# One written-out order of 1,100 steps, replaced by another, in a two-way attention followed by a two-layer network

## The chip, the core and the metric

The kernel runs on one core of one Trainium2 chip. The metric is the device time of one execution in microseconds (us). Five engines take part: TensorE (PE, matrix products, with its weight loads shown as PEld), VectorE (DVE), ScalarE (ACT), GpSimd (POOL), and SyncE (SP), which only issues transfers. Each engine runs its own queue strictly in the order of the program; where an instruction waits, all behind it in that queue wait too. Three runs of the kernel before took 209.22, 209.41 and 210.38 us, with a median of 209.41 us.

## The reference

```python
def _attn_ref(x, state):                     # x: 8 x 8 x 512 x 64, state: 8 x 8 x 32 x 64
    scale = 1.0 / np.sqrt(D)
    scores = scale * np.matmul(x, state.transpose(0, 1, 3, 2))
    a = softmax(scores)                      # over the 32 states
    xread = np.matmul(a, state)
    scores2 = scale * np.matmul(state, x.transpose(0, 1, 3, 2))
    a2 = softmax(scores2)                    # over the 512 tokens
    sread = np.matmul(a2, x)
    return np.concatenate([xread, sread], axis=2)

def reference(...):                          # rows: 8 x (512 + 32) = 4352, width 512
    x = attn_out.transpose(0, 2, 1, 3).reshape(B * S, H * D)
    h = x @ w_in                             # 512 x 2048
    g = np.maximum(h, 0.0) + alpha * np.minimum(h, 0.0)
    return g @ w_out                         # 2048 x 512
```

(`softmax` stands here for the lines that subtract the maximum, take the exponential and divide by the sum.)

## The kernel before

All work is cut into small steps, and one string, `ORDER`, lists them. A loop at the end of the kernel reads the string from front to back and calls the function of each step, so the list fixes the order of instructions on every engine at once. Nothing is moved by a scheduler afterwards. A step's name is followed by its numbers; a trailing letter names the engine (`a` ACT, `v` DVE, `p` POOL), and a trailing digit of a step on PE names the PSUM bank (0 to 5) that its result takes. Two more banks form one double tile called `two`.

The steps that matter here, with b a batch (0 to 7; 8 stands for the state rows of all batches together):

- `lst`, `wi`, `wo`, `lx`: transfers that POOL issues: the states, a quarter of `w_in` (512 columns), a quarter of `w_out` (512 rows), the tokens x of a batch. They convert 32-bit to 16-bit numbers on the way. x of batch 0 comes by transfers of SP and ACT instead, and `cx` casts it.
- `xt`/`xo`, `str`/`sro`: transposes on PE of x and of the states, and the copy out of PSUM. Later batches have `xd`, a transposing transfer on SP, in place of `xt`/`xo`.
- `tsc` or `sc`: scores on PE. `smax`, `ssh`, `sexp`, `ssum`, `snorm`, `wb`: the softmax over the states (largest of 32, subtract, exponential, sum and reciprocal, multiply, transpose back); for batch 0 in two halves, with `at`/`ao` (transposes on PE and copies) in place of `wb`. `tm`, `nb`, `te`, `tsum`, `tn`, `tt`: the softmax over the tokens, `rd`/`rdo` its product with x.
- `m.b.f`/`mo`: the states times a quarter f of `w_in`, on PE, and the copy to 16 bits. Since xread = a @ state, x @ w_in is got as a @ (state @ w_in).
- `F.b.jc`: 128 of the 2048 hidden columns for the 512 tokens of a batch (two matmuls 128x512; `f` the same in halves for the first two columns of batch 0). `N` on ACT takes relu(-h), `G` on DVE forms g = h + (1 - alpha) * relu(-h) (`n` and `g` for the halves).
- `S.0.q.j`/`O`: the second product of batch 0, in four PSUM banks. For batches 1 to 8 a product of 2x2 blocks with seven block products is used in place of eight: `W` (POOL, once) forms differences of blocks of `w_out`, `U.b.i.c` (POOL) sums and differences of blocks of g, `P.b.p.i.c` (PE) the seven products, `K` a copy of a partial sum from PSUM, `Q` the last addition or copy of an output block and its transfer by SP.
- `Z.k.n`: matmuls on a constant pattern whose result nobody reads; n counts 256 columns each. `fill(0, 16)` ahead of the list issues eight of 128x512.

What waits for what follows from the tiles. `F.b` needs the weights of its batch (`wb.b`, or `ao` for batch 0) and the `mo` of its quarter; `S` needs the `G` of two columns; `P` needs `G` or `U`; a step on PE that takes a bank waits until the last reader of what stood there is through.

Of the kernel before, what the change touches and what calls it, by code (L numbers as in the profile page):

```python
# [18 lines left out]
lst.0 cx.0.1.v cx.0.0.a xt.0.0.0.0 stc.a stt.1 cx.1.0.v sbd.1.a sto.a sbd.0.a xt.0.0.1.2 xt.0.1.0.3 xo.0.1.0.a  # L19
xo.0.0.0.v Z.4.3 xo.0.0.1.v tsc.0.1.4 cx.1.1.v tsc.0.0 smax.0.0 ssh.v.0.0 xt.0.1.1.5 xo.0.1.1.a sexp.0.0 tsc.1.0.0  # L20
Z.1.9 tsc.1.1 str.0.1 wi.0 m.0.0.2.3 sro.0.a Z.5.6 smax.0.1 ssh.v.0.1 Z.5.6 m.2.0.5.4 lx.1 sexp.0.1 m.1.0 mo.0.0.a.0
la mo.0.0.a.1 ssum.0.0 wi.1 mo.1.0.a ssum.0.1 wo.0 mo.2.0.v.1 snorm.p.0.0 xt.1.1.0.0 xt.1.0.0.1 xt.1.1.1.2 xo.1.1.0.a
xt.1.0.1.3 at.0.4 ao.0.a xo.1.0.0.v snorm.p.0.1 Z.1.3 xo.1.0.1.v oma.a xo.1.1.1.v at.1.1 sc.1 f.0.0.0.3 ao.1.a wi.2
F.0.3.0 F.0.2.2 m.0.1.4.1 mo.2.0.a.0 Z.5.3 n.0.0.0 f.0.0.1.5 N.0.3 mo.0.1.a.0 sb.1 tm.1 mo.0.1.a.1 F.0.7.4 F.0.5.1
N.0.2 g.0.0.0.1 g.0.0.0.0 G.0.2 n.0.0.1 G.0.3 g.0.0.1.1 nb.1.a te.1.0 g.0.0.1.0 N.0.7 N.0.5 F.0.6.3 G.0.7 smax.1
S.0.0.0.2 G.0.5 te.1.1 F.0.4.0 S.0.0.1 S.0.3.1.5 wo.1 wi.3 S.0.3.0 tsum.1 N.0.6 m.0.2 mo.0.2.a wo.2 S.0.1.1.4 wo.3
W.1.0.p G.0.6 S.0.1.0 m.1.1 F.0.10.1 N.0.4 G.0.4 mo.1.1.a N.0.10 G.0.10 F.0.8.3 S.0.1.3 S.0.1.2 ssh.p.1 sexp.1
F.0.9.0 ssum.1.s N.0.9 lx.2 xd.2 S.0.0.3 N.0.8 G.0.8 F.0.11.1 N.0.11 S.0.3.3 W.1.1.p snorm.p.1 m.0.3 mo.0.3.a S.0.3.2
# [5 lines left out]
sb.2 m.2.2.0.1 rd.1.2 mo.2.2.a.0 mo.2.2.a.1 rdo.1.a tm.2 S.0.3.7 tt.0 smax.2 S.0.3.5 O.0.3.a N.1.13 S.0.2.1.2 nb.2.a
S.0.2.5 te.2.1 S.0.2.6 S.0.2.7 te.2.0 F.1.1.0 N.1.1 G.1.13 F.1.8.1 N.1.8 G.1.0 G.1.1 F.1.4.5 S.0.2.2 m.3.2 G.1.8
N.1.4 G.1.4 F.1.10.0 lx.3 ssh.p.2 lst.1 sexp.2 mo.3.2.a ssum.2.1 tsum.2 S.0.2.4 S.0.2.0 F.1.9.5 rd.0.3 P.1.2.0.1.4
snorm.v.2 rdo.0.a N.1.9 G.1.9 S.0.2.3 N.1.10 P.1.1.0.1.3 P.1.1.1.1 P.1.2.1.1 xd.3 O.0.2.a tn.2.0.a m.2.3.1.2
mo.2.3.a.0 m.2.1 mo.2.3.a.1 wb.2 G.1.10 F.1.11.5 N.1.11 mo.2.1.a G.1.11 P.1.1.1.0 U.1.1.1.p str.1.1 sro.1.v tn.2.1.p
# [5 lines left out]
P.1.5.0.0 smax.3 P.1.7.1.1.4 F.2.10.1 N.2.10 F.2.5.0 N.2.5 G.2.5 G.2.10 F.2.4.2 N.2.4 G.2.4 te.3.1 P.1.5.1.1
U.1.3.0.p P.1.7.1.0 P.1.5.0.1 K.1.4.a U.1.4.1.p F.2.3.5 N.2.3 G.2.3 P.1.7.0.1 F.2.6.0 N.2.6 ssh.p.3 lx.5 F.2.12.1
N.2.12 G.2.6 P.1.7.0.0 P.1.3.1.0 m.6.0 Q.1.1.1 m.4.1.2.5 sexp.3 P.1.3.1.1 mo.6.0.a G.2.12 mo.4.1.a.0 ssum.3.0
U.2.1.0.p snorm.v.3 P.1.3.0.0 P.1.4.0.0 mo.4.1.a.1 P.1.3.0.1 U.2.2.0.p Q.1.0.1.a P.1.4.1.1 tsum.3 m.6.1.1.2 wb.3
mo.6.1.a.0 m.4.3 mo.4.3.a m.5.3.5.3 P.1.4.0.1 mo.5.3.a.1 P.2.1.0.1.1 P.2.1.1.0 P.1.4.1.0 mo.5.3.a.0 sc.4 U.2.1.1.p
# [772 lines left out]
```

## Time and profile before

| | |
|---|---|
| median of three runs | 209.41 us (209.22 to 210.38) |
| the profiled execution: span from its first to its last instruction | 207.1 us |
| PE busy | 200.4 us, 97% of the span |
| POOL busy | 179.5 us, 87% |
| DVE busy | 171.7 us, 83% |
| ACT busy | 155.3 us, 75% |
| first `F` with 512 columns (F.0.3) starts | 15.07 us |

The profile shows one execution, the span of which is given; its own time is not stated beside the span, so the 2.3 us between span and median are what lies around it. In a row of the timeline the columns are start, duration, engine, line, operation, output and inputs with their shapes, and the number of instructions merged into the row; a bracket tells how long the engine was idle before it, and for what. Matmul durations overlap: dense 128x512 matmuls start every 0.216 us though each is shown as 0.38 us long. "waited for" rows give total, times and longest.

### The profile page before, as it was taken

Reading aid. Unit: us, or ns where it says so; the run is one execution under the profiler, and the core shown is the slowest. Engines: PE = TensorE matmul, PEld = TensorE weight load, DVE = VectorE, ACT = ScalarE, POOL = GpSimd, SP = SyncE. Lnnn points to the kernel's source line nnn. Section 1 sums busy time; section 2 is a strip of 40 time slices with the busy share of each in tenths; the row PEclk is TensorE's granted clock in tenths of the full one; section 3 lists DMA queues with packets and bytes.
Section 4 is the critical chain, followed back from the end, with each engine's and each line's share of the span. In section 5 each row is a group of like instructions: output and inputs, shape, how many; then the busy total and the mean of one; then the engine's idle time right before and its main releaser. Section 6 shows DMA issues by size and latency. Waiting matters only on the chain.

```text
span 207.1 us, 5034 instructions
## 1 busy us (share of the span) xinstructions
PE 200.4 (97%) x1997; PEld 133.6 (65%) x1997; DVE 171.7 (83%) x251; ACT 155.3 (75%) x306; POOL 179.5 (87%) x113
## 2 busy tenths in 40 slices
PE   7899999999999999999999999999999999999992
PEld 2553344445566656687667856776877687788882
DVE  0889899999999999999999999999987967733231
ACT  4699999998999999997899787968755757502120
POOL 8177789997998999997997999797997999999960
PEclk9999999999999999999999999999999999999998
DMA  6999996698928798238976530126101200023223
GB/s 175 215 207 205 204 204 97 158 173 106 178 82 101 116 192 156 53 38 167 243 118 104 148 105 0 54 103 152 55 0 53 102 0 3 0 101 104 101 77 125
DMA packets 44038, 23.68 MB, mean 114 GB/s; under 512 B 22256, under 2 KB 43504, under 8 KB 44016
## 3 DMA queue, kind: packets, MB, share of 16 engines
q1 hardware_dynamic: 31152, 14.82, 28.4%
q0 software_dynamic: 11792, 8.09, 27.3%
q10 hardware_dynamic: 1072, 0.46, 0.9%
q8 instruction: 15, 0.25, 0.4%
q14 instruction: 7, 0.06, 0.1%
HBM read 17.31 MB, written 8.91 MB: 127 GB/s over the span
## 4 chain that ended last, share of the span: by engine, by line
PE 86%; DVE 5%; ACT 4%; DMA 2%; issue 1%; ACTq 0%
PE px L736 26%; PE h L577 24%; PE pv L736 13%; PE py L736 7%; PE m_ps L528 4%; PE h L586 3%; PE o L647 3%; DVE g L633 3%; DMA x<-in_x_dram 2%; PE sr_ps L501 2%; PE fill L253 2%; ACT neg L630 1%; PE sc L335 1%; ACT m L554 1%; PE xT_ps L320 1%
## 5 line engine op out<-in xcount | busy, mean ns | idle before, releaser
L633 DVE SCALAR_TENSOR_TENSOR g<-neg,oma_sb,h 128x512 f16<-128x512 f32 (+1 forms) x142 | 94.0, 711 | 11.6 <-ACT neg L630 11.0
L630 ACT ACTIVATE neg<-h 128x512 f32<-128x512 f32 (+1 forms) x142 | 75.6, 580 | 16.5 <-PE h L577 11.5
L577 PE MATMUL h<-aT,m 128*128 128x512 f16 x252 | 66.8, 380 | 0.1
L736 PEld LDWEIGHTS <-gsum 128*128 128x128 f16 x480 | 46.5, 98 | 13.1 <-issue 0.9
L736 PEld LDWEIGHTS <-g 128*128 128x128 f16 x360 | 34.7, 98 | 8.8 <-issue 1.4
L715 POOL TENSOR_TENSOR gsum<-g,g 128x1024 f16<-128x1024 f16 (+1 forms) x16 | 32.1, 2007 | 6.7 <-DVE g L633 4.9
L577 PEld LDWEIGHTS <-m 128*128 128x128 f16 x252 | 23.8, 98 | 18.4 <-issue 2.0
L715 POOL TENSOR_TENSOR gsum<-g,gsum 128x1024 f16<-128x1024 f16 (+1 forms) x16 | 32.0, 2005 | 1.5 <-PE px L736 1.0
L715 POOL TENSOR_TENSOR gsum<-gsum,g 128x1024 f16<-128x1024 f16 (+1 forms) x16 | 32.1, 2007 | 1.0
L736 PE MATMUL px<-ws,gsum 128*128 128x256 f16 x240 | 32.1, 273 | 0.0
L715 POOL TENSOR_TENSOR gsum<-g 128x1024 f16<-128x1024 f16 (+1 forms) x16 | 31.9, 2006 | 0.0
L752 ACT COPY kept<-px 128x512 f32<-128x512 f32 (+1 forms) x24 | 13.6, 567 | 21.0 <-PE px L736 20.9
L554 ACT CAST m<-m_ps 128x512 f16<-128x512 f32 x35 | 19.1, 602 | 1.5 <-PE m_ps L528 1.1
L769 DVE TENSOR_TENSOR oq<-pv,kept 128x512 f32<-128x512 f32 (+1 forms) x16 | 10.4, 649 | 10.6 <-PE pv L736 10.4
L736 PE MATMUL px<-w_out_sb,gsum 128*128 128x256 f16 x120 | 17.2, 273 | 0.0
L736 PE MATMUL px<-w_out_sb,g 128*128 128x256 f16 x120 | 17.2, 273 | 0.0
L405 POOL TENSOR_TENSOR ts<-ts,mx 128x1024 f32<-128x1024 f32 x7 | 13.3, 1911 | 4.4 <-DVE mx L400 4.4
L647 PE MATMUL o<-w_out_sb,g 128*128 128x512 f16 x64 | 16.6, 380 | 0.1
L736 PE MATMUL py<-w_out_sb,g 128*128 128x256 f16 x120 | 16.6, 273 | 0.0
L736 PE MATMUL pv<-ws,gsum 128*128 128x256 f16 x120 | 16.4, 273 | 0.0
L736 PE MATMUL pv<-ws,g 128*128 128x256 f16 x120 | 15.9, 273 | 0.0
L552 ACT CAST m<-m_ps 128x1024 f16<-128x1024 f32 x13 | 13.2, 1018 | 0.5 <-PE m_ps L528 0.4
(75 smaller groups left out, 238.1 us busy)
## 6 DMA issues: line engine op xcount, KB each, us to landing
out_dram<-oq SPq DMA_DIRECT2D x28, 256.0 KB, 2.6
xg<-in_x_dram POOLq DMA_DIRECT2D x7, 512.0 KB, 7.4
w_in_sb<-in_moe_w_in_dram POOLq DMA_DIRECT2D x4, 512.0 KB, 8.6
w_out_sb<-in_moe_w_out_dram POOLq DMA_DIRECT2D x4, 512.0 KB, 12.7
out_dram<-osb SPq DMA_DIRECT2D x4, 256.0 KB, 2.9
x<-in_x_dram SPq DMA_DIRECT2D x2, 256.0 KB, 3.7
out_dram<-oq SPq DMA_DIRECT2D x4, 128.0 KB, 2.1
x<-in_x_dram ACTq DMA_DIRECT2D x1, 256.0 KB, 4.6
```

The source lines that it names most:

```text
L405: engine(e).tensor_tensor(blocks(cols(live["ts", b], j, S)), blocks(scored(b, j)), over_blocks(cols(live["mx", b], j, S // N)), ALU.subtract,)
L528: nc.tensor.matmul(t[N * k : N * (k + 1), :], st_head(b, h)[64 * r : 64 * r + 64, :], w_in_sb[64 * r : 64 * r + 64, c, 512 * f : 512 * (f ...
L552: copier(e)(m_tile(b, f), t)
L554: copier(e)(m_tile(b, f)[:, g, :], t[g])
L577: nc.tensor.matmul(h.rearrange("p (r j s) -> p r j s", r=2, j=2), ms[b, f][:, g, 128 * j : 128 * (j + 1)], weights(b, g), start=(g == 0), ...
L630: nc.scalar.activation(neg, h, RELU, bias=0.0, scale=-1.0)
L633: nc.vector.scalar_tensor_tensor(g_tile(b, jc), negs.pop((b, jc)), oma_sb[:, jc : jc + 1], hs.pop((b, jc)), ALU.mult, ALU.add,)
L647: nc.tensor.matmul(outs[b, q], g_tile(b, jc)[:, 128 * q : 128 * (q + 1)], w_out_sb[:, jc, :], start=not begun and jc == 2 * jc2, stop=left ...
L715: engine(e).tensor_tensor(t, x(), y(), op)
L736: nc.tensor.matmul(pbanks[b, name][:, i, :], of(b, c)[:, j, 128 * i : 128 * (i + 1)], moving[:, 4 * c + j, :], start=not begun and j == 0, ...
L752: copier(e)(t, pbanks[b, "x"])
L769: nc.vector.tensor_tensor(osb, pbanks[b, name], kept[b, add], ALU.add)
```

## The change

Only the string `ORDER` differs: 1,107 steps before, 1,104 now. (It is a line shorter, so line numbers are one lower from there on.) Nearly every step stands at a new place, and most steps on PE that begin a result name another PSUM bank. Beside that:

- The fill steps `Z.4.3 Z.1.9 Z.5.6 Z.5.6 Z.1.3 Z.5.3` become `Z.3.6 Z.3.9 Z.3.6`. In instructions six matmuls 128x384 go; the ten of 128x512 and the one of 128x256 stay.
- Casts of x, batch 0: two move from DVE to ACT, `ao.0` from ACT to DVE. Two of the three `mo` copies on DVE move to ACT, and one other comes to DVE.
- Five of the `tn` scalings move from ACT to POOL and one back (nine on POOL now, five before). Four `K` copies, of batches 6, 7 and 8, move from ACT to DVE. Of the eight plain copies out (`Q.b.0.1`) one is on DVE now, before two.
- The PSUM bank in which `ssum` leaves its sums is another one for batches 2 to 7.
- POOL issues `wi.0` ahead of `lst.0`, `lx.2` ahead of `wo.3`, and all weight transfers ahead of `snorm.p.0.0`; `W.4.1` stands behind several sums `U.1`, before ahead of all of them.

```diff
 ORDER = """
-lst.0 cx.0.1.v cx.0.0.a xt.0.0.0.0 stc.a stt.1 cx.1.0.v sbd.1.a sto.a sbd.0.a xt.0.0.1.2 xt.0.1.0.3 xo.0.1.0.a
-xo.0.0.0.v Z.4.3 xo.0.0.1.v tsc.0.1.4 cx.1.1.v tsc.0.0 smax.0.0 ssh.v.0.0 xt.0.1.1.5 xo.0.1.1.a sexp.0.0 tsc.1.0.0
...
+stc.a cx.0.0.a xt.0.0.0.5 stt.0 wi.0 lst.0 cx.0.1.a lx.1 xo.0.0.0.v cx.1.0.a Z.3.6 xt.0.0.1.3 sbd.0.a sbd.1.a
+xo.0.0.1.v xt.0.1.0.5 tsc.0.0.4 xo.0.1.0.a cx.1.1.v tsc.0.1 xt.0.1.1.3 wi.1 smax.0.0 sto.a ssh.v.0.0 tsc.1.0.0
...
 Q.8.0.1.a P.8.4.0.0 Q.8.1.0
 """
```

Three places in the queues. POOL at the start, before: the transfers, the two halves of `snorm` of batch 0 (the row marked x2), further transfers, and the first `W`.

```order
L219 DMA st<-in_state_dram 128x448
L228 DMA w_in_sb<-in_moe_w_in_dram 128x4x512
L167 DMA xg_71<-in_x_dram 128x8x256
L202 MEMSET alpha_rows 128x32
L228 DMA w_in_sb<-in_moe_w_in_dram 128x4x512
L234 DMA w_out_sb<-in_moe_w_out_dram 128x4x512
L427 TENSOR_TENSOR an_155<-ts_152,r_0_154 128x512 [waits DVE_49,Activation_49] x2
L228 DMA w_in_sb<-in_moe_w_in_dram 128x4x512
L234 DMA w_out_sb<-in_moe_w_out_dram 128x4x512
```

And now, on POOL at the same place:

```order
L218 DMA st<-in_state_dram 128x448
L166 DMA xg_71<-in_x_dram 128x8x256
L227 DMA w_in_sb<-in_moe_w_in_dram 128x4x512
L233 DMA w_out_sb<-in_moe_w_out_dram 128x4x512
L227 DMA w_in_sb<-in_moe_w_in_dram 128x4x512
L201 MEMSET alpha_rows 128x32
L233 DMA w_out_sb<-in_moe_w_out_dram 128x4x512
L227 DMA w_in_sb<-in_moe_w_in_dram 128x4x512
L233 DMA w_out_sb<-in_moe_w_out_dram 128x4x512 [waits DMASW0_49]
L166 DMA xg_267<-in_x_dram 128x8x256 [waits DMASW1_49]
L233 DMA w_out_sb<-in_moe_w_out_dram 128x4x512 [waits DMASW2_49]
L426 TENSOR_TENSOR an_163<-ts_160,r_0_162 128x512 [waits DVE_49,Activation_49] x2
```

The first `w_in` transfer now stands one row above the first of these. Eleven transfers stand ahead of the two `snorm` halves where there were five. POOL's transfers take eight completion semaphores in turn (DMASW0 to 7), so the ninth to eleventh wait until the first, the second and the third transfer (the last of these x of batch 1, `xg_71`) have landed.

ACT from the first exponential of batch 0 (`ts`) to the copies of its weights (`aT`), before:

```order
L414 ACTIVATE ts_152<-ts_152 128x512 [waits DMAHW3_49,DVE_49]
L303 COPY stT<-st_ps_181 128x896 [waits PE_49]
L414 ACTIVATE ts_152<-ts_152 128x512 [waits DVE_49]
L554 CAST m_0_239<-m_ps_0_0_197 128x512 [waits PE_49]
L554 CAST m_0_239<-m_ps_0_1_198 128x512 [waits PE_49]
L552 CAST m_0_250<-m_ps_0_230 128x1024 [waits PE_49]
L325 COPY xT_273<-xT_ps_1_0_258 128x4x128 [waits PE_49]
L389 COPY aT_156<-at_ps_280 128x512 [waits PE_49]
L294 ACTIVATE oma_sb<-alpha_sb 128x16 [waits DVE_49]
L389 COPY aT_156<-at_ps_295 128x512 [waits PE_49]
```

And now, on ACT:

```order
L302 COPY stT<-st_ps_174 128x896 [waits PE_49]
L413 ACTIVATE ts_160<-ts_160 128x512 [waits DVE_49]
L553 CAST m_0_238<-m_ps_0_0_196 128x512 [waits PE_49]
L413 ACTIVATE ts_160<-ts_160 128x512 [waits DVE_49]
L553 CAST m_0_238<-m_ps_0_1_197 128x512 [waits PE_49]
L551 CAST m_0_264<-m_ps_0_219 128x1024 [waits PE_49]
L324 COPY xT_276<-xT_ps_1_0_240 128x4x128 [waits PE_49]
L553 CAST m_0_278<-m_ps_0_1_251 128x512 [waits PE_49]
L553 CAST m_0_278<-m_ps_0_0_250 128x512
L293 ACTIVATE oma_sb<-alpha_sb 128x16 [waits DVE_49]
L553 CAST m_1_333<-m_ps_1_0_307 128x512 [waits PE_49]
L388 COPY aT_164<-at_ps_319 128x512 [waits PE_49]
```

The copy of the transposed states (`stT`) now precedes the first exponential; three more casts of `m` stand ahead of the last copy of `aT`, and one of the two `aT` copies has gone to DVE.

POOL in the stretch in which the first blocks of `w_out` are combined (`ws`), before:

```order
L691 TENSOR_TENSOR ws_430<-w_out_sb 128x1024 [waits DMASW6_49]
L427 TENSOR_TENSOR an_357<-ts_355,r_1_468 128x1024 [waits DVE_49,Activation_49]
L691 TENSOR_TENSOR ws_563<-w_out_sb,ws_430 128x1024 [waits DMASW0_49]
L691 TENSOR_TENSOR ws_570<-w_out_sb,ws_563 128x1024 [waits Pool_49]
L482 TENSOR_SCALAR e_0_575<-e_0_575,r_0_576 128x512 [waits DVE_49]
```

And now, on POOL:

```order
L690 TENSOR_TENSOR ws_421<-w_out_sb 128x1024 [waits DMASW6_49]
L690 TENSOR_TENSOR ws_421<-w_out_sb 128x1024 [waits DMASW4_49]
L426 TENSOR_TENSOR an_352<-ts_350,r_1_449 128x1024 [waits DVE_49,Activation_49]
L481 TENSOR_SCALAR e_1_372<-e_1_372,r_1_373 128x512 [waits DVE_49]
L690 TENSOR_TENSOR ws_567<-w_out_sb,ws_421 128x1024 [waits DMASW0_49,Pool_49]
```

A scaling of the other softmax (`e`) of batch 1 has come in between; ACT did it before. Batch 0's (`e_0`) follows further down, in both lists.

More of the change, by code (lines that the diff above doesn't have):

```diff
@@ L24 @@
[L24 to L28, printed above, removed]
@@ L34 @@
[L34 to L38, printed above, removed]
@@ L44 @@
[L44 to L48, printed above, removed]
@@ new lines @@
+xo.0.0.1.v xt.0.1.0.5 tsc.0.0.4 xo.0.1.0.a cx.1.1.v tsc.0.1 xt.0.1.1.3 wi.1 smax.0.0 sto.a ssh.v.0.0 tsc.1.0.0
+xo.0.1.1.a str.0.1 sro.0.a tsc.1.1 smax.0.1 sexp.0.0 m.0.0.2.4 Z.3.9 wo.0 wi.2 la m.1.0 xt.1.0.0.1 wo.1 wi.3 ssh.v.0.1
+ssum.0.0 mo.0.0.a.0 xt.1.1.0.0 xt.1.1.1.5 m.2.0.2.3 sexp.0.1 mo.0.0.a.1 ssum.0.1 mo.1.0.a wo.2 lx.2 xt.1.0.1.4 wo.3
+snorm.p.0.0 xo.1.1.0.a mo.2.0.a.1 xo.1.0.0.v xo.1.0.1.v xo.1.1.1.v snorm.p.0.1 at.0.1 sc.1 ao.0.v m.0.1.0.1 mo.2.0.a.0
+lst.1 at.1.4 f.0.0.0.2 oma.a tm.1 mo.0.1.a.0 ao.1.a n.0.0.0 nb.1.a Z.3.6 mo.0.1.a.1 F.0.3.4 F.0.2.0 sb.1 g.0.0.0.1
```

134 lines of the change are left out of this document (72 added, 62 removed).

## The prediction

> **What bounds the kernel now.** I read the page first, for its busy times and the chain that ended last, then the windows, because the start and the long middle have different limits.
>
> ```profile
> span 207.1 us, 5034 instructions
> PE 200.4 (97%) x1997; PEld 133.6 (65%) x1997; DVE 171.7 (83%) x251; ACT 155.3 (75%) x306; POOL 179.5 (87%) x113
> ...
> PE 86%; DVE 5%; ACT 4%; DMA 2%; issue 1%; ACTq 0%
> ```
>
> ```profile
> 0.00:15.00 15.00, 12.62 (x141) 6.58 (x142) 8.48 (x19) 9.90 (x19) 8.75 (x18) 1.00 1.09 198
> 15.00:32.00 17.00, 16.52 (x133) 6.81 (x131) 15.79 (x24) 16.58 (x32) 13.78 (x11) 1.00 1.27 205
> 32.00:48.00 16.00, 15.87 (x141) 6.78 (x140) 15.41 (x22) 15.55 (x32) 14.34 (x10) 1.00 0.76 140
> 48.00:75.00 27.00, 27.00 (x345) 17.42 (x344) 26.53 (x37) 25.75 (x50) 25.96 (x15) 1.00 0.79 119
> ...
> 175.00:198.00 23.00, 23.00 (x208) 20.00 (x206) 9.95 (x17) 6.44 (x14) 22.18 (x15) 1.00 0.20 70
> ```
>
> PE is 97% busy and carries 86% of the chain. The columns of the windows are length, then the busy time of PE, PEld, DVE, ACT and POOL, the granted clock, the share and rate of the transfers. The first 15 us are a chain of transfers and softmax steps of batch 0 in which PE has gaps. From 15 to 48 us ACT (16.58 of 17, 15.55 of 16) and DVE (15.79, 15.41) are as full as PE. After that PE never stops. A new order can therefore win only what PE still waits or works for nothing, and can lose more than that.
>
> Matmuls overlap in the profile, so I measure PE in slots, from start to start:
>
> ```profile
> 15.07 1.03 PE L577 MATMUL h<-aT,m 128*128 128x512 f16 x4
> ...
> 16.03 0.41 PE L528 MATMUL m_ps<-w_in_sb,stT 64*32 64x512 f16 x8
> 16.37 0.50 PE L253 MATMUL fill<-pattern 128*128 128x384 f16 x2
> ```
>
> ```profile
> 40.88 0.68 PE L501 MATMUL sr_ps<-e2T,xg 128*64 128x32 f16 x32
> 41.49 2.98 PE L647 MATMUL o<-w_out_sb,g 128*128 128x512 f16 x12
> 44.30 1.46 PE L577 MATMUL h<-aT,m 128*128 128x512 f16 x6
> 45.60 0.59 PE L647 MATMUL o<-w_out_sb,g 128*128 128x512 f16 x2
> ...
> 49.87 1.04 PE L736 MATMUL px<-w_out_sb,g 128*128 128x256 f16 x8
> 50.75 0.60 PE L736 MATMUL py<-w_out_sb,g 128*128 128x256 f16 x4
> 51.28 0.63 PE L528 MATMUL m_ps<-w_in_sb,stT 64*32 64x512 f16 x16
> 51.84 0.61 PE L577 MATMUL h<-aT,m 128*128 128x512 f16 x2
> ```
>
> An F or S takes 0.43 us (six matmuls from 44.30 to 45.60), a P 0.44 (eight from 49.87 to 50.75), an `rd` 0.53 and 0.61 with the change that follows (40.88 to 41.49). One `m` and the change behind it take 0.34 (16.03 to 16.37), two and a change 0.56 (51.28 to 51.84): about 0.23 for an `m`, and 0.1 for each change between these packed products and full ones. Twelve matmuls of S from 41.49 should take 2.59 and take 2.81: a wait of 0.2 that no idle row shows.
>
> **The start: F.0.3 comes 1.6 us later.** Two transfers are exchanged (`wi.0` ahead of `lst.0`). These are POOL's first issues and, in the same order, their time from issue to landing (the last column):
>
> ```profile
> 2.11 0.76 POOL L219 DMA_DIRECT2D st<-in_state_dram  x1
> 2.88 0.77 POOL L228 DMA_DIRECT2D w_in_sb<-in_moe_w_in_dram  x1
> 3.63 0.90 POOL L167 DMA_DIRECT2D xg<-in_x_dram  x1
> ```
>
> ```profile
> st<-in_state_dram POOLq DMA_DIRECT2D x1, 112.0 KB, 4.9
> w_in_sb<-in_moe_w_in_dram POOLq DMA_DIRECT2D x1, 512.0 KB, 6.7
> xg<-in_x_dram POOLq DMA_DIRECT2D x1, 512.0 KB, 8.6
> ```
>
> They land at 7.0, 9.6 and 12.2 us, one behind the other, 512 KB each 2.6 us. The windows show 198 and 205 GB/s up to 32 us without a break, so earlier issue does not bring weights earlier; only the exchange counts. The states now land when both are in, at 9.6, and the last token scores of batch 0 stand behind their transposes on PE. ACT's queue up to the weights of batch 0, before:
>
> ```profile
> 9.10 0.58 PE L269 MATMUL st_ps<-ident,st 128*64 128x128 f16 x14
> ...
> 9.21 0.63 ACT L414 ACTIVATE ts<-ts 128x512 f32<-128x512 f32 x1 [0.63 <-DVE ts L405]
> 9.74 0.89 ACT L303 COPY stT<-st_ps 128x896 f16<-128x896 f16 x1
> ...
> 11.65 2.06 POOL L427 TENSOR_TENSOR an<-ts,r 128x512 f16<-128x512 f32 x2 [5.54 <-DVE r L424]
> 12.39 1.01 ACT L552 CAST m<-m_ps 128x1024 f16<-128x1024 f32 x1 [0.15 <-PE m_ps L528]
> 13.30 0.59 ACT L325 COPY xT<-xT_ps 128x512 f16<-128x512 f16 x1
> 13.77 0.61 ACT L389 COPY aT<-at_ps 128x512 f16<-128x512 f16 x1
> 14.25 0.24 ACT L294 ACTIVATE oma_sb<-alpha_sb 128x16 f32<-128x16 f32 x1
> 14.39 0.58 ACT L389 COPY aT<-at_ps 128x512 f16<-128x512 f16 x1
> ```
>
> ACT starts the next instruction 0.48 us after one of 512 columns, 0.53 after an exponential, 0.91 after 1024, 0.14 after `oma`. Now `str.0` runs from 9.6 to 10.1, its copy (0.89) ends at 11.0, and the first exponential starts there instead of at 9.21. Behind it stand, in the new order, `mo`, exponential, `mo`, `mo` of 1024, `xo`, two `mo`, `oma`, `mo`, `ao.1`: 0.53 + 0.48 + 0.53 + 0.48 + 0.91 + 3 x 0.48 + 0.14 + 0.48 = 5.0. `ao.1` starts at 16.0 and ends at 16.6; F.0.3 starts at 16.65 against 15.07: **+1.58**. POOL reaches nearly as far: its eleventh transfer waits for the third to land (12.2), takes 0.8, and the two `snorm` (2.06) end at 15.1, from which `ao.1` could start at 15.5. Queued behind that wait are only these and `lst.1`. Six fills are gone, but up to here they covered PE's gaps, so they cost and save nothing there.
>
> **PE's list from F.0.3 to F.1.11 is shorter.** `m.0.1` (16.03 to 16.37) is ahead of F.0.3 now, the fill at 16.37 (0.50) is gone, and four P, an F, an `m` and an `rd` stand behind F.1.11 instead of ahead. Counting the list in slots: before 62 of F, f and S (26.7), 4 P (1.75), 10 m (2.3), 3 sc (0.7, each taken as an `m`), 2 rd (1.05), a fill (0.43), 22 changes (2.2): 35.1 us. It took 51.84 - 15.07 = 36.77, so 1.67 are waits. Now 61 (26.3), 8 m (1.8), 3 sc (0.7), 1 rd (0.5), 16 changes (1.6): 30.9 us.
>
> The waits in it now come from walking on along the queues. An exponential over the tokens takes ACT 0.7; the second G of the second row is G.0.4:
>
> ```profile
> L464 ACT ACTIVATE e<-sc,nb 128x512 f16<-128x512 f32 x16 | 11.1, 696 | 0.2
> ...
> 22.71 1.43 DVE L633 SCALAR_TENSOR_TENSOR g<-neg,oma_sb,h 128x512 f16<-128x512 f32 x2
> ```
>
> Behind `ao.1` ACT has `n`, `nb`, `mo`, N.0.3, N.0.2, `n`, two `te`, N.0.7, N.0.5, N.0.6 and `mo.0.2`: 16.0 + 0.48 + 5 x 0.48 + 0.2 + 2 x 0.7 + 3 x 0.48 + 0.91 = 22.8, where N.0.4 starts (0.6); G.0.4 (0.74) then ends at 24.2. Before it ends at 24.1, with the same F and S issued by then. So most of the late start is made up, since ACT and DVE were the limit there already. PE waits about 0.2 for `wi.2` and 0.2 for `wi.3` (at 2.6 us a transfer and a little more they land near 20.7 and 25.8), 0.4 at S.0.3.1 for DVE (the halves `g` in bank 5 stand behind a `smax`), and 0.2 in small pieces: **1.0**, with bounds 0.3 and 2.0. `lx.2` is issued ahead of `wo.3`, so the transposed x for `sc.2` comes sooner and `wo.3` later, near 33.5; S.0.1.7 reaches it at 34. F.1.11 starts at 16.65 + 30.9 + 1.0 = 48.55.
>
> **Behind F.1.11** before took 203.39 - 51.84 = 151.55:
>
> ```profile
> 202.35 1.04 PE L736 MATMUL pv<-ws,g 128*128 128x256 f16 x8
> ```
>
> Now 4 P, an F, an m, an rd and two changes more: 3.1. PE's last matmul ends at 48.55 + 151.55 + 3.1 = 203.2: **-0.2**. The 0.9 us of waits inside the 151.55 (its slots: 97 F 41.8, 192 P 83.9, 30 F and P of batch 8 13.1, 19 `m`, 6 `rd`, 5 `sc` and `str` 9.1, 26 changes 2.6, in all 150.5, and 0.2 of the last matmul's tail) I take as equal, with bounds 0 and 2.5. The tail behind it, an addition and a transfer, is the same.
>
> The moved copies cost nothing there: four `K` on DVE at some 0.69 against 0.60 on ACT lie in a stretch where DVE works 9.95 of 23 us; K.7.4 makes G.8.10 wait, whose sum U.8.1.0 is needed 2 us later. Without that cover it would be 0.1 each. Bank numbers move no work; a wrong one is a wait, and that is inside the bounds. The net four scalings on POOL are the rival below.
>
> Sum against the execution of 207.1: 206.9; with the same 2.3 us around it **209.3** against the median of 209.41. Within 0.5% (1.05 us) is about what a measurement of this kernel can tell from no change.
>
> **Rivals.**
>
> *POOL falls behind (slower).*
>
> ```profile
> L482 POOL TENSOR_SCALAR e<-e,r 128x512 f16<-128x512 f16 x5 | 3.5, 690 | 0.3 <-DVE r L474 0.3
> 76.58 2.13 POOL L715 TENSOR_TENSOR gsum<-gsum,g 128x1024 f16<-128x1024 f16 x1
> 79.94 1.04 PE L736 MATMUL px<-ws,gsum 128*128 128x256 f16 x8
> ```
>
> Four scalings are 2.8 us on an engine with 1 us free in 48 to 75. U.2.2.1 ends 1.2 us ahead of its product (78.71, 79.94). In the new order, with 2.1 us a sum, 0.7 a scaling and 0.9 a transfer in POOL's queue against PE's slots, I find such margins down to some 0.3 us (U.1.2.0 to P.1.6.0, U.4.2.0 to P.4.6.1). It decides once DVE hands over g more than 0.3 us late there: then each later sum is late too, up to 2.8 - 1.2 = 1.6 us: 210.9. For it: POOL has no row that makes up time; against it: `W.4.1` (2.1 us) now stands later. Chance 0.2.
>
> *The list has fewer waits (faster).* Of 1.0 and 0.9 us assumed, 1.9 can go, to 207.4; half gives 208.3. For it: by DVE's spacing its margins after 50 us are 0.3 us wider than before; against: the start. Chance 0.21.
>
> *The late start is not made up (same or slower).* PE's waits stay 1.67 and later ones grow by 0.5: 210.5. Chance 0.05.
>
> *PE's clock falls.* With fills gone, PE idles up to 1.5 us at a time between 8 and 13 us, waiting for the states; the granted clock was 1.00 in the first window. At half clock a slot doubles: over the eight slots from F.0.3 to S.0.0.1 that costs 8 x 0.43 = 3.4 us, half of it behind DVE, which is the limit there: 1.7 are left, 211.0. Chance 0.02. The Trainium skill, TensorE: Matmul & The Clock Gate, section "What's actually happening", says that the clock halves after an idle window of about 3.4 us. By that rule a gap of 1.5 us does not do it, and the 1.00 of the first window, in which PE was idle for 2.4 us in pieces, agrees.
>
> **How the numbers follow.** No change within 0.5% has 0.52; faster 0.21; slower 0.20 + 0.05 + 0.02 = 0.27. The range runs from 207.9, where the faster rival has all but a half microsecond of its gain, to 211.0, POOL's end.
>
> **What would show it.** The second profile should show the copy `stT<-st_ps` near 10.2, F.0.3 near 16.6, and G.0.4 ending near 24.2; the weight transfers still landing 2.6 us apart; F.1.11 near 48.5; no idle PE after 50 us, and rows "POOL gsum <- DVE g" of about 5 us as now. The forecast is wrong if rows of PE waiting for POOL's `gsum` appear, if F.0.3 starts after 17.2, or if the span moves by over 1 us while these marks hold.

## The result and the profile after

The changed kernel takes 211.32 us (median of 210.62 to 212.75), the kernel before 209.38 in the same measurement (209.22 to 210.38): a ratio of 1.0106, 95% interval [1.0079, 1.0132]. It is slower by 1%, where 209.3 had been forecast. The profiled execution is the longest of the four, 212.75 us with a span of 210.9. Its page, in the parts shown of before:

```profile
span 210.9 us, 5025 instructions
PE 200.4 (95%) x1991; PEld 133.9 (64%) x1991; DVE 172.7 (82%) x252; ACT 151.9 (72%) x301; POOL 181.7 (86%) x117
...
PEclk9969999999999999999999999999999999999999
...
PE 82%; DMA 9%; DVE 4%; POOL 2%; issue 0%; ACT 0%; DVEq 0%; POOLq 0%; ACTq 0%
```

and its windows, in the stretches shown of before:

```profile
0.00:15.00 15.00, 11.25 (x94) 5.46 (x94) 5.98 (x12) 9.22 (x17) 10.79 (x21) 0.90 1.08 194
15.00:32.00 17.00, 16.20 (x162) 7.31 (x161) 15.56 (x26) 16.18 (x32) 10.88 (x9) 0.98 1.27 205
32.00:48.00 16.00, 16.00 (x138) 7.06 (x137) 15.59 (x23) 14.89 (x33) 14.42 (x10) 1.00 0.72 124
48.00:75.00 27.00, 25.93 (x331) 15.77 (x329) 25.39 (x36) 25.11 (x49) 25.22 (x15) 1.00 0.79 139
...
175.00:198.00 23.00, 23.00 (x207) 20.05 (x206) 12.26 (x23) 8.88 (x21) 21.65 (x12) 1.00 0.11 39
```

Transfers are on 9% of the chain that ended last, against 2% before. The clock (the column after POOL's, and the PEclk row) falls near 13 us: 0.90 in the first window. And from 48 to 75 us, where PE was busy without a break before, 1.07 us are missing. PE's longest waits, but for that of the first fill at the program's start:

```profile
PE st_ps L268 <- DMA st<-in_state_dram: 1.9, 1, 1.9
PE sr_ps L500 <- DMA e2T<-e: 1.5, 2, 1.1
...
PE h L576 <- DVE g L632: 0.5, 1, 0.5
PE o L646 <- DVE g L617: 0.4, 1, 0.4
```

The first is the states' transfer at the start. The second is new: twice the state reads (`sr_ps`) wait for the transposed token weights `e2T`, 1.1 us before those of batch 2 and 0.4 before those of batch 5. The third is F.6.5, a product of batch 6. Here are the rows of PE at the start and at the reads of batch 2:

```profile
10.53 0.58 PE L268 MATMUL st_ps<-ident,st 128*64 128x128 f16 x14 [1.91 <-DMA st<-in_state_dram]
...
18.86 1.03 PE L576 MATMUL h<-aT,m 128*128 128x512 f16 x4
...
50.29 0.61 PE L576 MATMUL h<-aT,m 128*128 128x512 f16 x2
...
61.59 0.68 PE L500 MATMUL sr_ps<-e2T,xg 128*64 128x32 f16 x32 [1.07 <-DMA e2T<-e]
```

F.0.3 starts at 18.86 (forecast 16.65) and F.1.11 at 50.29 (forecast 48.55).

### The profile page after: what moved, and what is told of

The parts are those of the page before. It is cut to its first block, busy times and chain, and to the rows that moved or that the text cites. A ratio compares the mean times of both kernels' runs of the same rounds, so it can differ in the third digit from the quotient of the medians.

```text
span 210.9 us, 5025 instructions
## 1 busy us (share of the span) xinstructions
PE 200.4 (95%) x1991; PEld 133.9 (64%) x1991; DVE 172.7 (82%) x252; ACT 151.9 (72%) x301; POOL 181.7 (86%) x117
## 4 chain that ended last, share of the span: by engine, by line
PE 82%; DMA 9%; DVE 4%; POOL 2%; issue 0%; ACT 0%; DVEq 0%; POOLq 0%; ACTq 0%
PE px L735 23%; PE h L576 22%; PE pv L735 12%; PE o L646 6%; DMA e2T<-e 6%; PE py L735 5%; PE m_ps L527 4%; DMA st<-in_state_dram 4%; PE h L585 3%; PE sr_ps L500 2%; DVE g L632 1%; PE sc L334 1%; PE xT_ps L319 1%; PE fill L252 1%; DVE g L617 1%; DVE nb L446 1%
## 5 line engine op out<-in xcount | busy, mean ns | idle before, releaser
L576 PE MATMUL h<-aT,m 128*128 128x512 f16 x252 | 67.7, 379 | 0.5 <-DVE g L632 0.5
L576 PEld LDWEIGHTS <-m 128*128 128x128 f16 x252 | 24.3, 98 | 17.0 <-issue 1.2
L553 ACT CAST m<-m_ps 128x512 f16<-128x512 f32 x36 | 20.3, 605 | 2.8 <-PE m_ps L527 2.7
L751 ACT COPY kept<-px 128x512 f32<-128x512 f32 (+1 forms) x20 | 11.7, 585 | 12.0 <-PE px L735 11.9
L735 PE MATMUL px<-w_out_sb,g 128*128 128x256 f16 x120 | 16.7, 273 | 0.0
L735 PE MATMUL pv<-ws,g 128*128 128x256 f16 x120 | 16.7, 273 | 0.0
L735 PE MATMUL px<-w_out_sb,gsum 128*128 128x256 f16 x120 | 16.4, 273 | 0.0
```

Source lines behind the costliest of these rows:

```text
L553: copier(e)(m_tile(b, f)[:, g, :], t[g])
L576: nc.tensor.matmul(h.rearrange("p (r j s) -> p r j s", r=2, j=2), ms[b, f][:, g, 128 * j : 128 * (j + 1)], weights(b, g), start=(g == 0), ...
L735: nc.tensor.matmul(pbanks[b, name][:, i, :], of(b, c)[:, j, 128 * i : 128 * (i + 1)], moving[:, 4 * c + j, :], start=not begun and j == 0, ...
L751: copier(e)(t, pbanks[b, "x"])
```

## The experiments

Three theories of the loss stand against each other. *Start*: the exchange of the states' and the first weights' transfers makes the first 17 us longer and this lasts to the end. *Collision*: two loads of x that the new list issues earlier or later run beside transposing transfers of the token weights and stretch them; PE waits at the state reads. *Clock*: PE's idle time ahead of the states' transposes lets its clock be halved. The forecast's own view, that a late start is made up by 50 us, is the rival of the first. All times of before below are from the same measurement as the run beside them: 209.09 us in the first four, 209.16, 209.11 and 209.12 in the later ones.

**The changed kernel once more.** No edit.

> The changed kernel once more. Its profiled execution (212.75 us) had half a clock between 10.5 and 17 us and was 1.2 to 2.1 us longer than its other executions. If the halved clock is the cause of the loss, a profile with the full clock shows F.0.3 near 17 us and a span near 207.5, and the time moves with it; if the late states and the late transposed weights of batches 2 and 5 are the cause, F.0.3 still starts after 17 at full clock, the waits of 1.2 us before the state reads of batch 2 and of 0.6 before those of batch 5 are there again, and the time is 211.0 to 211.5.

It took 211.69 us (211.01 to 213.35, ratio 1.0132 [1.0103, 1.0160]). This time the profiled execution was the shortest, at full clock, with a span of 209.1:

```profile
10.00:18.00 8.00, 7.21 (x105) 3.94 (x106) 6.87 (x14) 7.44 (x15) 4.55 (x6) 1.00 1.30 203
```

```profile
9.93 0.58 PE L268 MATMUL st_ps<-ident,st 128*64 128x128 f16 x14 [1.38 <-DMA st<-in_state_dram]
...
14.80 0.40 PE L385 MATMUL at_ps<-ident,an 128*128 128x128 f16 x4 [0.61 <-POOL an L426]
...
17.36 1.03 PE L576 MATMUL h<-aT,m 128*128 128x512 f16 x4
...
48.70 0.60 PE L576 MATMUL h<-aT,m 128*128 128x512 f16 x2
...
60.01 0.68 PE L500 MATMUL sr_ps<-e2T,xg 128*64 128x32 f16 x32 [1.08 <-DMA e2T<-e]
...
105.85 1.19 PE L500 MATMUL sr_ps<-e2T,xg 128*64 128x32 f16 x64 [0.24 <-DMA e2T<-e]
```

The same window of the first profile of the changed kernel, where PE had waited 1.91 us, stands at 0.79 of the clock:

```profile
10.00:18.00 8.00, 7.08 (x98) 3.83 (x99) 5.33 (x12) 6.08 (x12) 4.99 (x6) 0.79 1.31 205
```

So the two profiles separate the theories. At full clock F.1.11 is 0.15 us off the forecast (48.70 against 48.55), though F.0.3 was 0.7 late. All the rest of the loss lies behind it: a span of 209.1 against the forecast 206.9, of which 0.15 is ahead of F.1.11. In the first profile F.1.11 stands a further 1.59 us later, and the span is 1.8 longer. Of the 1.59, 0.60 is that the states landed later in that execution (transposes at 10.53 against 9.93). The other 0.99 lies between the transposes and F.1.11 (39.76 against 38.77 us). There the clock was halved, for nearly all of these 3.5 us:

```profile
12.00:15.50 3.50, 3.50 (x32) 1.69 (x30) 2.77 (x7) 3.47 (x7) 2.06 (x3) 0.52 1.26 207
```

**The states first.** The exchange is undone in the changed kernel:

```diff
-stc.a cx.0.0.a xt.0.0.0.5 stt.0 wi.0 lst.0 cx.0.1.a lx.1
+stc.a cx.0.0.a xt.0.0.0.5 stt.0 lst.0 wi.0 cx.0.1.a lx.1
```

> The changed kernel with the states' transfer ahead of the first weights again, all else as changed. If the exchange is what makes the start late, the first copy of the states starts near 8.5 instead of 11.15, the first exponential near 9.3 instead of 11.95, F.0.3 near 16 instead of 18.9, and of 211.3 us 1.6 to 2.5 go: 208.8 to 209.7. If the late start is made up behind it by ACT and DVE, as the prediction had it, G.0.4 moves by under 0.5 us and the time stays at 210.9 to 211.4. The wait before the state reads of batch 2 stays at 1 us or more either way.

211.06 us (210.90 to 211.23, ratio 1.0096 [1.0082, 1.0111]). The states' transposes started at 8.44, the first exponential at 9.87, yet F.0.3 only at 17.07 and F.1.11 at 48.49: 0.2 us better than with the exchange at full clock, not 1.6. (A later profile with the same start, that of the edit at F.6.5 below, has 17.34 and 48.78, so one profile of each does not tell 0.2 or 0.3 us from no difference.) The expectation of the start theory fell. POOL holds the start instead. In this profile as in the one before, the first transposes of batch 0's weights (`at`) wait for POOL's normalisation, and from there PE's own steps, the fill Z.3.6 last, take 2.56 us to F.0.3 (14.80 to 17.36, and here):

```profile
14.51 0.40 PE L385 MATMUL at_ps<-ident,an 128*128 128x128 f16 x4 [0.61 <-POOL an L426]
...
17.07 1.03 PE L576 MATMUL h<-aT,m 128*128 128x512 f16 x4
```

POOL's rows:

```profile
9.94 0.89 POOL L166 DMA_DIRECT2D xg<-in_x_dram  x1 [0.88 <-DMA w_in_sb<-in_moe_w_in_dram]
12.62 0.75 POOL L233 DMA_DIRECT2D w_out_sb<-in_moe_w_out_dram  x1 [1.79 <-DVE r L423]
13.39 2.06 POOL L426 TENSOR_TENSOR an<-ts,r 128x512 f16<-128x512 f32 x2
```

The eleventh transfer is issued at 12.62, and the normalisations of batch 0 (`an`) follow it at 13.39. The tenth is let go by the landing of the first weights (first row). The eleventh's row puts its wait down to DVE's `r`, but in the queue this transfer waits only for the third one, that of x, which ends near 12.3 (issued at 3.6, 8.7 us to landing); the profiles of the changed kernel name that transfer in the same place, and a later run shows that the normalisations can start at 11.73. The exchange's price lies in the spread: 210.9 to 211.2 without it (four executions), 210.6 to 213.4 with it (ten, in two measurements).

**Two loads of x moved.** In the changed kernel:

```diff
-P.1.1.1.0 N.1.10 P.1.2.1.1.4 wb.2 rdo.0.a F.2.0.2 tn.2.0.a lx.4 mo.2.1.a
+P.1.1.1.0 N.1.10 P.1.2.1.1.4 wb.2 rdo.0.a F.2.0.2 tn.2.0.a mo.2.1.a
...
-U.1.2.0.p m.5.0.5.4
+U.1.2.0.p lx.4 m.5.0.5.4
...
-P.1.3.0.1 Q.1.1.1 P.1.3.1.1
+P.1.3.0.1 xd.4 Q.1.1.1 P.1.3.1.1
...
-U.2.4.0.p P.2.7.1.0 tsum.4
+U.2.4.0.p lx.6 P.2.7.1.0 tsum.4
```

(`xd.4`, which transposes that x, leaves its place behind `m.3.0`, and `lx.6` its place behind `G.3.14`.)

> The changed kernel with two loads of x moved on POOL's queue: that of batch 4 three sums later (and its transposed copy behind the state reads of batch 2), that of batch 6 two steps earlier. If a load in flight beside the transposing transfer of the token weights is what makes that transfer take 5.7 and 6.3 us instead of 2.8, both fall to about 3 us, PE's waits of 1.24 and 0.58 us at the state reads go, and the time falls by 1.2 to 1.8 us to 209.5 to 210.1. If the transfer is late for another reason (issue or its queue), it stays above 5 us and the time at 211.0 to 211.5; if the waits go but are given back at the next limit, the time falls by under 0.5.

209.73 us (209.34 to 212.54, ratio 1.0043 [1.0024, 1.0062]). The time from issue to landing of batch 2's transposing transfer, first in the repeated changed kernel, then here:

```profile
DMA to landing us min/median/max: 5.7/5.7/5.7
```

```profile
DMA to landing us min/median/max: 2.8/2.8/2.8
```

For batches 4 and 5 the longest fell from 6.6 to 4.8; the one of 4.8 was issued at 97.56, when no load of POOL was in flight (the last had landed near 96.6), so a load is not the only thing that stretches such a transfer. The reads of batch 2 now follow the scores without a wait:

```profile
58.68 0.40 PE L334 MATMUL sc<-xT,stT 64*32 64x256 f16 x16
59.02 0.68 PE L500 MATMUL sr_ps<-e2T,xg 128*64 128x32 f16 x32
```

The two waits are gone and nothing gave them back: the span is 207.8 against 209.1, though F.1.11 started 0.16 later. This is the collision theory's number, 1.46 us behind F.1.11. The run moves two loads and one transposing transfer of x together, so it does not say how much each is worth.

**Both edits.**

> Both of these edits. If the late start and the two late transposing transfers are separate causes, their gains add: 211.3 - 1.6 - 1.5 = 208.2 us, with F.1.11 near 48.7 and no wait above 0.3 us at a state read. If one hides the other (the start's gain makes the token weights come earlier into the load), the gain is that of the larger alone: 209.5.

209.27 us (209.11 to 209.55, ratio 1.0009 [1.0001, 1.0018]): within 0.1% of the kernel before. These rows serve for the next run too:

```profile
17.05 1.03 PE L576 MATMUL h<-aT,m 128*128 128x512 f16 x4
...
21.03 0.41 PE L527 MATMUL m_ps<-w_in_sb,stT 64*32 64x512 f16 x8
...
48.39 0.60 PE L576 MATMUL h<-aT,m 128*128 128x512 f16 x2
```

F.1.11 starts at 48.39, PE's last product 1.78 us earlier than in the repeated changed kernel: 1.47 behind F.1.11 from the loads, 0.31 ahead of it from the start. The gains add, but the start's, as far as two profiles tell, is a fifth of what the expectation had put on it.

**The last early transfers behind the normalisations**, added to both edits:

```diff
-ssum.0.1 mo.1.0.a wo.2 lx.2 xt.1.0.1.4 wo.3 snorm.p.0.0 xo.1.1.0.a
+ssum.0.1 mo.1.0.a xt.1.0.1.4 snorm.p.0.0 xo.1.1.0.a
...
-snorm.p.0.1 at.0.1
+snorm.p.0.1 wo.2 lx.2 wo.3 at.0.1
```

> The kernel with both edits (states first, two loads of x moved), and now also the last three early transfers (wo.2, lx.2, wo.3) behind the two normalisations of batch 0 on POOL instead of ahead of them. In the kernel with both edits the last of them is issued at 12.60 us, after the third transfer has landed, and holds the normalisations to 13.37 although their sums are ready at 12.63. If that holds the start up, they start near 12.65, at.0 near 13.8 instead of 14.49 and F.0.3 near 16.4 instead of 17.05. If the late start is made up behind it, because ACT and DVE are the limit up to 34 us, F.1.11 still starts at 48.2 to 48.4 and the time is 209.0 to 209.3, against 209.27; if it is not made up, 208.5.

209.16 us (208.98 to 209.33, ratio 0.9991 [0.9973, 1.0009]). The normalisations start at 11.73 and F.0.3 at 16.66, 0.39 earlier, and F.1.11 at 48.38 as in the kernel with both edits. The 0.39 us went into a new wait for weights: the `m` that needs `wi.2`, a transfer issued at 6.0 in both, starts at 21.04 here and at 21.03 with both edits:

```profile
11.73 2.05 POOL L426 TENSOR_TENSOR an<-ts,r 128x512 f16<-128x512 f32 x2 [3.42 <-DVE r L423]
```

```profile
16.66 1.03 PE L576 MATMUL h<-aT,m 128*128 128x512 f16 x4
...
21.04 0.41 PE L527 MATMUL m_ps<-w_in_sb,stT 64*32 64x512 f16 x8 [0.26 <-DMA w_in_sb<-in_moe_w_in_dram]
...
48.38 0.60 PE L576 MATMUL h<-aT,m 128*128 128x512 f16 x2
```

Over all profiles of the changed list and its edits, F.1.11 starts 31.34 to 31.44 us behind F.0.3 wherever the three transfers stand in their place: eight profiles, with F.0.3 from 17.05 to 18.86. There a later start costs all of itself. With the three transfers moved it is 31.72 here, and in the two runs that also move them (all four edits, below) 31.63 with F.0.3 at 17.15 and 31.69 with it at 16.66. So the lead gained before 17.05 is lost again, here at `wi.2`; but all three profiles have the moved transfers, and no run starts earlier without moving them.

**DVE's order ahead of F.6.5**, added to both edits:

```diff
-F.5.6.3 sb.7 Q.4.0.1.a F.5.15.4 P.4.4.1.0 tsum.7 N.5.6 G.5.5 F.6.12.0 G.5.13 N.5.15 P.4.4.0.1 N.6.12 F.6.14.1 G.5.6
+F.5.6.3 G.5.5 sb.7 Q.4.0.1.a F.5.15.4 P.4.4.1.0 N.5.6 F.6.12.0 G.5.13 N.5.15 P.4.4.0.1 N.6.12 F.6.14.1 G.5.6 tsum.7
```

> The kernel with both edits, and on DVE G.5.5 ahead of the scores' step sb.7, and the sum tsum.7 behind G.5.6, instead of all three scaled blocks behind both. In the changed kernel DVE stands still for 0.9 us ahead of sb.7, which waits for an exponential, then spends 1.4 us on it and the sum, and F.6.5, which needs the PSUM bank that G.5.6 reads, starts 0.66 us late. If that order is the cause, the wait goes and the time falls by 0.65 to 208.6; if PE is then held by the next block or by POOL's sums of block 5, by under 0.3 us.

208.70 us (208.51 to 209.94, ratio 0.9978 [0.9955, 1.0002]). DVE and PE at that place in the repeated changed kernel:

```profile
137.43 1.25 DVE L366 STREAM_TRANSPOSE ts<-sc 128x1024 f32<-128x1024 f32 x1 [0.93 <-ACT e L463]
138.61 0.12 DVE L473 RECIPROCAL r<-r 128x2 f32<-128x2 f32 x1
138.65 3.36 DVE L632 SCALAR_TENSOR_TENSOR g<-neg,oma_sb,h 128x512 f16<-128x512 f32 x5
```

```profile
140.74 0.59 PE L576 MATMUL h<-aT,m 128*128 128x512 f16 x2 [0.49 <-DVE g L632]
```

With one scaled block ahead of the transpose the row of PE's wait is gone, F.6.5 starts 0.64 us earlier counted from F.1.11, and the time fell by 0.57. That wait was a third loss of the new list.

**One part of the change alone in the kernel before:**

```diff
-lst.0 cx.0.1.v cx.0.0.a
+wi.0 lst.0 cx.0.1.v cx.0.0.a
```

(the first weights' `wi.0` taken from its place behind the states' transposes).

> The kernel before with one part of the change alone: the first weights' transfer ahead of the states'. The states then land near 9.6 to 10 instead of 7.0, their transposes start near 10 instead of 9.10. If only the start is late and is made up while ACT and DVE are the limit, F.0.3 starts 0.5 to 1 us later, F.1.11 under 0.3 us later and the time is 209.1 to 209.4; if the idle PE also lets its clock fall in some executions, single times of 210 to 212 us appear, with a granted clock below 0.995; if the late start is not made up, all are near 210.

209.70 us (209.52 to 210.38, ratio 1.0028 [1.0013, 1.0044]). In the profiled execution PE waited for the states, F.0.3 came 1.16 us later than before, and F.1.11 1.16 later:

```profile
10.30 0.58 PE L269 MATMUL st_ps<-ident,st 128*64 128x128 f16 x14 [0.93 <-DMA st<-in_state_dram]
...
16.23 1.03 PE L577 MATMUL h<-aT,m 128*128 128x512 f16 x4
...
53.00 0.61 PE L577 MATMUL h<-aT,m 128*128 128x512 f16 x2
```

In this execution of the old list nothing is made up: from F.0.3 to F.1.11 it takes 36.77 us, as before. But it is one of the longer ones, 210.04 us; the median is only 0.54 above the kernel before. In the other executions the start was less late or part of it was made up, and no profile shows which. In the profiles of the new list the exchange moves F.0.3 by some 0.3 us or less, because POOL holds it nearly as long. All twelve executions kept the clock at 0.997 or more; PE was idle for 0.9 us at a time in the profiled one, not 1.4 or more.

**A fill against the idle time**, first in the changed kernel, then in the one with the two loads moved:

```diff
-ssh.v.0.0 tsc.1.0.0 xo.0.1.1.a str.0.1
+ssh.v.0.0 tsc.1.0.0 Z.2.14 xo.0.1.1.a str.0.1
```

> The changed kernel with 1.5 us of fill on PE ahead of the states' transposes, where PE otherwise idles for 1.4 to 2 us; nothing else moved. If PE's idle time is what lets the clock be halved in some executions, all executions now agree within 0.4 us at a granted clock of 0.996 or more, and the median falls from 211.3 to 211.7 to the 211.0 of the full clock. If the spread has another cause (the transfers, ACT), single times of 212 us and more remain.

> The changed kernel with the two loads of x moved, and 1.5 us of fill on PE ahead of the states' transposes. Without the fill 4 of 10 executions had a granted clock of 0.992 or less and took 210.6 to 212.5 us, the other six 209.3 to 209.7 at 0.996 or more. If PE's idle time there is what lets the clock be halved, none has a clock below 0.995 now and all are between 209.3 and 209.9; if it has another cause, again about 4 of 10 are above 210.5.

With the fill, the changed kernel took 211.28 us (211.12 to 211.93) and the other 209.68 (209.56 to 210.06, ratio 1.0032 [1.0020, 1.0045]). None of the ten executions had a mean clock below 0.996; without the fill, 8 of 20 executions of these two and the first measurement stood at 0.984 to 0.992, and all 8 were longer than the shortest of their measurement, seven by 1.0 to 2.3 us and one by 3.2. (If the fill changed nothing, ten executions without a fallen clock out of these thirty would come up about once in 46 draws.) The medians fell by 0.4 and 0.05. Against the executions at full clock without the fill, whose medians are 211.2 and 209.5, the fill costs 0.1 to 0.15 us; in the second kernel PE goes straight from it into the states' transposes (8.43 + 1.67 = 10.1, where they start at 10.06), so it may delay them a little. The expectation that all agree within 0.4 us held but for one execution of the first (211.93 at a clock of 1.00), which stays unexplained.

**All four edits together**, and the same with four copies back on ACT.

> All four edits together: states first, two loads of x moved, the last three early transfers behind the normalisations, the order of DVE around block 5's last scaled products. If the edit at F.6.5 is worth its 0.65 us and the later transfers are worth nothing at full clock, 208.5 to 208.7, a little under the kernel before (209.16); if the earlier start is worth something now that less waits behind it, 208.2.

```diff
-K.6.4.v
+K.6.4.a
...
-K.7.4.v
+K.7.4.a
...
-K.8.1.v
+K.8.1.a
...
-K.8.4.v
+K.8.4.a
```

> The same, with the four copies K.6.4, K.7.4, K.8.1 and K.8.4 on ACT again, as they were before the change. If moving them to DVE costs nothing, as the prediction had it, within 0.2 us of the run with all four edits; if the copy on DVE delays a scaled product that PE needs, 0.1 to 0.4 us faster than it.

208.56 us (208.37 to 208.95, ratio 0.9967 [0.9950, 0.9983]) and 208.65 (208.42 to 208.73, ratio 0.9976 [0.9966, 0.9986]). Both are faster than the kernel before by some 0.5 us, which is about what can be told from no change, and do not differ: the copies on DVE cost nothing, as forecast. The spans of the first are 206.5 to 207.1 us, about the forecast's 206.9: with the added waits gone, what is left of its sum is right. That the gain is part of what the new list saves on PE (35.1 - 30.9 - 3.1 = 1.1 us of slots in the prediction's count) fits, but was not taken apart.

**The collision in the kernel before.** A first try moved the load of batch 4's x ahead by two sums:

```diff
-U.1.2.1.p P.1.6.1.1 N.2.11 F.2.2.5
+U.1.2.1.p lx.4 P.1.6.1.1 N.2.11 F.2.2.5
```

> The kernel before with the load of x of batch 4 alone moved ahead by two sums on POOL, so that it starts near 54.9 us, just ahead of the transposing transfer of batch 2's token weights at 55.1. If the load beside it is what stretches that transfer, it lands after 5.7 us instead of 2.8, PE waits 1.5 us at the state reads of batch 2 (now at 59.2), and the time is 210.5 to 210.8 instead of 209.16. If the length came from the place in SP's queue or another thing of the changed order, the transfer still lands after 3 us and the time stays.

It told little: 210.24 us, but from 208.91 to 215.71 (ratio 1.0030 [1.0004, 1.0055]). In the profiled execution SP issued the transposing transfer at 53.60, ahead of the load at 55.18; it landed after 4.0 us and nobody waited. So the load was put one sum further ahead, where it is always first:

```diff
-U.1.3.1.p mo.3.0.a.0 U.1.2.1.p
+U.1.3.1.p lx.4 mo.3.0.a.0 U.1.2.1.p
```

> The kernel before with the load of x of batch 4 three sums earlier on POOL, so that it starts near 52.8 us, ahead of the transposing transfer of batch 2's token weights, which SP issues between 53.6 and 55.1; SP's queue is as before. If a load in flight beside it stretches the transfer, it lands 5 us or more after its issue, near 59.5 to 60.8, PE waits 0.3 to 1.5 us at the state reads of batch 2 and the time is 209.5 to 210.6. If the transfer takes under 4 us although the load is in flight, it is not the load, the reads start at 59.2 and the time is 209.1.

213.88 us (212.55 to 215.17, ratio 1.0220 [1.0178, 1.0262]), slower than any expectation. Load, transfer, its time to landing and PE:

```profile
53.13 0.96 POOL L167 DMA_DIRECT2D xg<-in_x_dram  x1
```

```profile
53.52 2.35 SPq L486 DMA_TRANSPOSE e2T<-e  x1
```

```profile
DMA to landing us min/median/max: 8.0/8.0/8.0
```

```profile
61.60 0.68 PE L501 MATMUL sr_ps<-e2T,xg 128*64 128x32 f16 x32 [1.95 <-DMA e2T<-e]
...
63.05 1.89 PE L736 MATMUL px<-ws,gsum 128*128 128x256 f16 x8
```

```profile
62.00:70.00 8.00, 8.00 (x86) 4.65 (x80) 5.78 (x8) 6.04 (x14) 4.89 (x3) 0.79 0.55 68
```

With a load 0.4 us ahead of it the transfer took 8.0 us, where it took 4.0 in the first try, with the load 1.6 us behind it, and 2.8 in the kernel before. That is the collision in the old list, by one move, with SP's queue in its order. All profiles agree: this transfer took 2.7 to 3.0 us in the nine with no load beside it, and 5.7 to 5.8 in the four with one issued 1.7 us ahead. And behind PE's wait of 1.95 us its clock is halved: eight matmuls of P are shown as 1.89 us where eight took 1.04, and from them to the end of the three F behind it takes 3.75 us (63.05 to 66.80) where the kernel before takes 2.17 (60.78 to 62.95), 1.6 more. The wait and the slower clock make up the 3.6 us that the profiled execution, 212.71 us, is longer than the kernel before; what the longer ones lost beyond it no profile shows. Each of its six executions had a mean clock of 0.988 to 0.992.

## Why the prediction was wrong, point by point

- **Its sum failed in the term of the waits behind F.1.11**, "the 0.9 us of waits inside the 151.55 (...) I take as equal, with bounds 0 and 2.5". At full clock PE goes from F.1.11 at 48.70 to the end of its last product at 205.20: 156.5 us, where the forecast had 151.55 + 3.1. So 2.75 us of waits stand where 0.9 were taken, beyond the upper bound. Three new ones come to 2.1 (from start to start, less the slot): 1.15 at the reads of batch 2, 0.3 at those of batch 5 and 0.65 at F.6.5. Nothing in the working followed the transfers behind 50 us: the load of batch 4 moves ahead of the transposing transfer (from 61.33 to 54.07, beside a transfer issued at 55.13 and then at 55.75), and that could be read in the new order. Moving two loads, and in the other list one, showed the cause at batch 2; at batch 5 the wait went in the same run. The third wait was DVE's order, which one edit took away.
- **The 2.3 us around the span** were too many. The median of 209.41 and the span of 207.1 belong to different executions; wherever both are on record for one (209.09 and 207.3 for the kernel before, 211.01 and 209.1 for the changed one), 1.8 to 1.9 us lie around it. The forecast span of 206.9 is then 208.7 to 208.8 us, not 209.3, so the sum was some 0.5 us further off than the time shows.
- **The start** came late by another path than the one forecast. The first steps were right (the states' transposes at 9.93, forecast 9.6; the first exponential at 11.36, forecast 11.0). But F.0.3 at 17.36 (16.65) was not set by ACT's queue: PE comes to it from the transposes at 14.80, which wait for POOL, by its own steps, the last of which is a fill. The forecast had taken the fills there as free. With the states first, ACT's exponential is 1.5 us earlier and F.0.3 only 0.3. "If F.0.3 starts after 17.2", named as a sign of being wrong, was met, but it is not what made the forecast wrong.
- **F.1.11 at 48.70 (48.55) was near by luck.** F.0.3 was 0.7 us late, and the stretch from there to F.1.11 took 31.34 us where 30.9 + 1.0 had been forecast, 0.6 less. "So most of the late start is made up" held against the old list (G.0.4 ended at 24.66, forecast 24.2, before 24.1), but the reason given, that ACT and DVE were the limit there already, is not borne out. In the eight profiles of the new list above a later F.0.3 is passed on in full, and in the profiled execution of the old list with the exchange nothing is made up either. The new list's stretch is shorter; it does not absorb the start.
- **POOL**, called nearly as late as ACT, was the later of the two: its eleventh issue waits for the third landing and holds the normalisations (12.62 and 13.39 even with the states first). Taking that away brought F.0.3 0.39 us ahead and F.1.11 nothing.
- **Weights no earlier for an earlier issue** was right: 194 to 206 GB/s up to 32 us in both lists.
- **The copies on DVE and the scalings on POOL** cost nothing: the run with the copies moved back is equal, and no row has PE's matmuls waiting for POOL's `gsum` in the changed kernel. The slower rival, POOL, did not happen; POOL waited longer for g (9.3 us in 6 waits, against 4.9 in 4), where 5 had been forecast.
- **The falling clock, given a chance of 0.02**, happened in 8 of 20 executions of the list with the exchange, and its price of 1.7 us was too high there: of the 1.8 us between the two profiles about 1.0 is the clock's and 0.6 the later landing of the states. Where PE was the limit, in the last run, it was 1.6. The forecast had PE idle for at most 1.5 us at a time; it was 1.38 in the profile at full clock and 1.91 in the other, because the states landed later. The Trainium skill, TensorE: Matmul & The Clock Gate, section "What's actually happening", names an idle window of about 3.4 us that runs freely. That the same kernel falls in some executions and not in others agrees with a free-running window, though the idle time differed too (1.38 and 1.91); that 1.9 us of idle time are enough does not agree with 3.4, and the measurement decides.
- **"No idle PE after 50 us"** was the mark that told: 1.08 us at 60.01 and 0.49 at 140.74.

What stays open: two of twelve executions of the kernel with DVE's order changed also had a clock of 0.992, with the states first, and no profile caught one; nor is there a second profile of the changed kernel with a fallen clock, so how long PE was idle in the other seven executions is not known. Why a load beside it stretches the transposing transfer was not measured. The Trainium skill, DMA: Bandwidth & Descriptors, section "SWDGE vs HWDGE vs iDMA", says that transfers issued by GpSimd and by the other engines feed different queues of the same 16 engines, which serve them in turn; that would give a stretch of this kind, but no run here takes the queues apart.

## What to carry to other kernels

When an order is changed, follow every transfer against every other, also where PE is the bound: a load moved by 7 us beside a short transposing transfer cost more than all that the new list saved on PE. A start that comes later or earlier is worth only what no other wait behind it hides, so read it from the waits that follow, list by list and in more than one profile. And an idle stretch of nearly 2 us on PE cost twice in the two profiles that have one, once as a wait and once as a halved clock behind it; a fill in that place cost 0.1 to 0.15 us.

## What was not expected of the hardware

- A transposing transfer of 128x1024 16-bit values on SP's queue, that of batch 2, landed after 2.7 to 3.0 us in the nine profiles with no load of POOL beside it. It took 5.7 to 5.8 in the four with a 512 KB load issued 1.7 us ahead of it, 4.0 with one issued 1.6 us behind it, and 8.0 with one issued 0.4 us ahead.
- PE's clock was halved after 1.91 and 1.95 us of idle time, and not after 1.38, 1.08, 1.03 or 0.93. Read from windows of half a microsecond, it fell 1.6 and 1.3 us after PE had begun to work again (near 12.1 and 62.9 us), and it stayed at half for 3.4 us in both profiles. The second one in those 3.5 us:

```profile
62.75:66.25 3.50, 3.50 (x28) 1.80 (x13) 2.93 (x3) 2.18 (x5) 3.50 (x2) 0.52 1.19 143
```
